# Attention and a mixture of experts on one core: 128-row operands for the first two fp32 score products, Relu on ScalarE, and a new order of steps

## The chip, the cores and the metric

The kernel runs on one core of one Trainium2 chip. The core has a matrix engine (TensorE, PE in the profile, with its weight loads shown apart as PEld), a vector engine (VectorE, DVE), an activation engine (ScalarE, ACT), a general engine (GpSimd, POOL) and an engine that issues the DMA transfers (SyncE, SP). Each works through a queue of its own in order and waits on semaphores for the others. The metric is the time of one execution in microseconds on the device; lower is better. TensorE's clock is gated: the profile gives the granted share of full speed.

## The reference

Eight batches of eight heads, 576 positions, 64 numbers per head. First an attention with a bias from running sums, then on its output a mixture of four experts, each with an attention of its own; the two best experts of a position are added up.

```python
scores = scale * np.matmul(q, k.transpose(0, 1, 3, 2))
s_pos = np.maximum(s, 0.0)
cum = np.cumsum(s_pos, axis=-1)
bias = -(cum[:, :, :, None] - cum[:, :, None, :])
scores = np.where(causal, -1000000000.0, scores + np.minimum(bias, 0.0))
attn = softmax(scores)          # with the maximum taken off first
x = attn @ v                    # heads side by side: 8 x 576 x 512
...
logits = x @ w_gate
for e in range(E):              # E = 4
    q, k, v = x @ wq[e], x @ wk[e], x @ wv[e]
    ye = causal_softmax(scale * q @ k.T) @ v @ wo[e]
    # added to out with the gate's weight where e is one of the two best
```

All numbers are fp32.

## The kernel before

**Slots.** The work is cut into pairs of heads (or of experts). A pair is a slot n; there are 48 and two empty ones, N = 50. The first four slots are the four head pairs of batch 0. From batch 1 on each batch brings four attention slots and two expert slots of the batch before.

**What a slot does.** q and k come transposed, 64 numbers on 64 partitions. Below them stand helper rows: three rows with the running sums of Relu(s) on the side of k against rows of ones on the side of q, so that the product adds the bias, and one row with minus the maximum of each query. The steps have short names, which the list ORDER uses as `slot:step`:

- `m0` to `m5` (function `maxima`, L730): bf16 products mx of 64 queries with the keys, in six PSUM banks; `M0` to `M5` (L744): VectorE reduces them to the maxima (its by-product goes to the tile sink, which nobody uses). `mt` (L764) turns the maxima with a TensorE transpose, `mA` (L768) copies them on ScalarE, `mq` (L774) sends them by DMA into the minus-maximum row of q.
- `s0` to `s5`, `s6` (function `scores`): the score products, keys as weights. From slot 2 on they are split into two rounded products (L799 on 128 rows, L804 on 97). Slots 0 and 1, the list DIRECT, take the raw fp32 q and k in one product of 68 rows (64 of q and k, 3 of sums, 1 of minus maximum) from a tile `whole` (L793, and L831 for the tails of 64 keys): this needs none of the splitting (`l0` to `l3`, `h0` to `h3`, `lq`, `lk`) with which the other slots begin.
- `E0` to `E6`: exp on ScalarE; `b`, `d`: causal masks and row sums on GpSimd; `v`, `V`: products with v (L910) and their copy.

**Before the first slot.** `c0` loads s, `c1` takes Relu and scales (L451, on VectorE), `c2` scans, `c3` and `c4` split the sums into three bf16 parts (L463, L466). `hc` sends them into the helper rows of a slot (two transfers for a slot of DIRECT, L630), `cu` to DRAM for later slots. `i0` to `i39` are spare TensorE products (L1372): they multiply the tile sink with itself and nobody reads the result. GpSimd fills constants: `k1`, `q1` the helper rows of `whole`, `f00` to `f22` those of the split tiles, `ca`, `id`, `lc` masks and the identity.

**What sets the order.** The program is written out once, with no loop at run time: `order` reads ORDER from left to right and each step issues its instructions to the engines' queues at that place. PSUM has eight banks that are taken and given back in the order of this list, and a tile's buffers are reused in the same order, so the list decides both the place in each queue and which waits there are.

The functions that the change touches, and what calls them:

Of the kernel before, what the change touches and what calls it, by code (L numbers as in the profile page):

```python
# [13 lines left out]
OP = mybir.AluOpType  # L14
# [25 lines left out]
def pieces(kt, q0, q1):  # L40
# [280 lines left out]
)  # L321

def order(pairs):
    for x in ORDER.split():
        n, step = x.split(":")
        yield int(n), step


COPY_Q, COPY_K = 3, 9
DIRECT = (0, 1)
RX = 67
SPARE = 40

FB = [0, 8, 10, 12]
NQK1 = 2
NQK2 = 3
RC = 96
RM = 96  # L340


@with_exitstack
def tile_attention_then_moe(ctx, tc, qk, vm, vt, s, wqk, wvg, wo, out):
    nc = tc.nc
# [1130 lines left out]
```

## Time and profile before

| | |
|---|---|
| median of 3 runs | 678.92 us (678.58 to 679.16) |
| profiled execution | 679.76 us, span of its instructions 677.9 us |
| busy share of the span | PE 97%, DVE 77%, ACT 69%, POOL 62% |
| mean granted TensorE clock | 0.970 |
| DMA | 81.23 MB, mean 120 GB/s |

The span runs from the first to the last instruction. A row of a timeline gives start, length, engine, line, operation, output and inputs; a group of like instructions in a row has its count behind an x. A row of windows gives the stretch, its length, for each engine the busy time in it and the count, and then the granted clock, the share of the DMA engines and GB/s. Lines are those of the kernel before.

### The profile page before, as it was taken

To read this page: it belongs to the slowest core of one execution; us is meant where nothing else is said; L and a number is where in the kernel's file an instruction comes from. 1 tells how busy PE (TensorE), PEld (TensorE's weight loads), DVE (VectorE), ACT (ScalarE), POOL (GpSimd) and SP (SyncE) were. 2 spreads that over 40 slices of the span, in tenths; PEclk is the share of its full clock that TensorE was granted. 3 is DMA by queue.
4 is the path that set the end of the run, shared out by engine and by line. 5 is a ranking of instruction groups with operands and counts; after the bars stand their busy time and mean duration, and the time that the engine had idled before them with its cause. 6 is when DMAs were issued, how large, how long until landed. Compare 5 with 4: busy or idle time off the path is not lost.

```text
span 677.9 us, 16595 instructions
## 1 busy us (share of the span) xinstructions
PE 658.2 (97%) x5906; PEld 539.1 (80%) x5906; DVE 525.1 (77%) x1449; ACT 470.8 (69%) x1090; POOL 417.9 (62%) x557
## 2 busy tenths in 40 slices
PE   6789999999999999999999989999999999999997
PEld 2456778878987888878887878888888888889885
DVE  6387787788978867986689867889677976773894
ACT  2166978787678686777677846888667876675573
POOL 7069858768766648755868537758757665808130
PEclk9559999999999999999999989999999999999999
DMA  4513544433544535555446343637363544331413
GB/s 96 164 54 108 167 134 118 109 104 96 144 109 136 146 92 144 139 172 141 120 129 160 107 124 108 175 107 157 89 193 92 137 126 111 75 84 51 121 33 124
DMA packets 48917, 81.23 MB, mean 120 GB/s; under 512 B 19246, under 2 KB 19246, under 8 KB 48836
## 3 DMA queue, kind: packets, MB, share of 16 engines
q1 hardware_dynamic: 48836, 80.18, 44.6%
q8 instruction: 47, 0.77, 0.5%
q14 instruction: 34, 0.28, 0.1%
HBM read 44.55 MB, written 10.09 MB: 81 GB/s over the span
## 4 chain that ended last, share of the span: by engine, by line
PE 85%; ACT 5%; DVE 3%; DMA 3%; issue 1%; SPq 1%; ACTq 0%; DVEq 0%
PE pvp L910 18%; PE pq L1140 13%; PE s L799 11%; PE s L804 10%; PE mx L730 8%; PE pw L1140 8%; PE po L1140 7%; PE sm L963 4%; PE s L793 2%; PE s L841 1%; ACT k L673 1%; PE po L1114 1%; ACT p L820 1%; DVE s_r L451 1%; DVE sink L744 1%
## 5 line engine op out<-in xcount | busy, mean ns | idle before, releaser
L744 DVE CUSTOM_DVE_ANT_0 sink<-mx,mask 128x64 bf16<-128x64 f32 (+7 forms) x432 | 168.9, 428 | 61.7 <-PE mx L730 50.7
L820 ACT ACTIVATE p<-s 128x512 f32<-128x512 f32 x288 | 160.1, 590 | 49.7 <-PE s L804 31.1
L853 POOL TENSOR_SCALAR_AFFINE_SELECT p<-p 128x256 f32<-128x256 f32 (+1 forms) x192 | 95.6, 507 | 157.6 <-ACT p L820 130.9
L799 PE MATMUL s<-q,k 128*128 128x320 f32 (+2 forms) x552 | 153.1, 301 | 1.2 <-DMA q<-q 0.6
L804 PE MATMUL s<-q,k 97*128 97x320 f32 (+2 forms) x552 | 141.7, 291 | 0.2 <-DMA q<-mr 0.2
L874 POOL TENSOR_TENSOR r<-r,p 128x640 f32<-128x640 f32 x92 | 129.6, 1409 | 4.5
L799 PEld LDWEIGHTS s<-q,k 128*128 128x128 f32 x552 | 105.4, 191 | 13.7 <-issue 5.0
L704 DVE TENSOR_TENSOR q<-raw,q 64x576 fp32r<-64x576 f32 x92 | 87.3, 962 | 31.4 <-ACT q L669 13.5
L1140 PE MATMUL pq<-x,wqkh 128*128 128x288 f32 x512 | 106.8, 302 | 1.8 <-ACT raw L1158 1.8
L804 PEld LDWEIGHTS s<-q,k 97*128 97x128 f32 x552 | 105.4, 191 | 1.0 <-DMA q<-mr 0.5
L910 PE MATMUL pvp<-p,v 128*64 128x320 f32 (+3 forms) x1024 | 102.9, 325 | 0.0
L730 PE MATMUL mx<-k,q 96*64 96x512 bf16 (+7 forms) x920 | 90.2, 298 | 0.4 <-ACT q L669 0.3
L710 DVE TENSOR_TENSOR k<-raw,k 64x1024 fp32r<-64x1024 f32 (+1 forms) x92 | 80.9, 890 | 12.3 <-DMA k<-k 6.7
L1140 PEld LDWEIGHTS pq<-x,wqkh 128*128 128x128 f32 x512 | 81.9, 190 | 3.9 <-ACT raw L1158 2.0
L910 PEld LDWEIGHTS pvp<-p,v 128*64 128x64 f32 x1024 | 63.1, 137 | 21.1 <-issue 2.4
L1140 PE MATMUL pq<-x,wqkl 128*128 128x288 f32 x256 | 75.9, 296 | 0.0
L871 POOL TENSOR_TENSOR r<-p 128x384 f32<-128x384 f32 x46 | 50.2, 1092 | 28.2 <-ACT p L820 28.2
L730 PEld LDWEIGHTS <-q 96*64 96x64 bf16 x920 | 47.4, 112 | 24.6 <-issue 9.2
L673 ACT ACTIVATE k<-raw 64x1024 fp32r<-64x1024 f32 (+1 forms) x92 | 61.9, 680 | 6.8 <-DMA raw<-in_qk_dram 5.1
L669 ACT ACTIVATE q<-raw 64x576 fp32r<-64x576 f32 x92 | 62.0, 679 | 0.9
L924 ACT ACTIVATE pv<-pvp 128x256 f32<-128x256 f32 (+1 forms) x92 | 36.7, 405 | 25.0 <-PE pvp L910 24.6
L1140 PE MATMUL pw<-wvgh,x 128*128 128x260 f32 x256 | 51.8, 288 | 0.0
(140 smaller groups left out, 1172.5 us busy)
## 6 DMA issues: line engine op xcount, KB each, us to landing
raw<-in_qk_dram SPq DMA_DIRECT2D x30, 576.0 KB
rb<-rr SPq DMA_DIRECT2D x92, 144.0 KB
q<-q SPq DMA_DIRECT2D x45, 288.0 KB
k<-k SPq DMA_DIRECT2D x39, 288.0 KB
v<-in_vm_dram SPq DMA_DIRECT2D x32, 256.0 KB
out_dram<-o SPq DMA_DIRECT2D x32, 256.0 KB
q<-mr SPq DMA_DIRECT2D x92, 2.2 KB
whole<-in_qk_dram SPq DMA_DIRECT2D x8, 144.0 KB
```

The costliest lines, as they stand in the source:

```text
L673: nc.scalar.activation(part(k2[0:64]), get_raw(n)[64:128, :, k], AF.Copy)
L704: nc.vector.tensor_tensor(a[64:128, j], get_raw(n)[0:64, j], q2[0:64, j].bitcast(F32), op=OP.subtract)
L710: nc.vector.tensor_tensor(part(c[0:64]), get_raw(n)[64:128, :, k], part(c[64:128]).bitcast(F32), op=OP.subtract)
L730: nc.tensor.matmul(t[64 * j : 64 * j + 64, c0 : c0 + k1 - k0], q2[0:rc, 64 * qt : 64 * qt + 64], keys(n, rc, j, k0, k1).bitcast(BF16)[:, 1 ...
L744: nc.vector.tensor_tensor_reduce(sink[:, c0 : c0 + w], t[:, c0 : c0 + w], mask[:, m0 : m0 + w], scale=1.0, scalar=mcol[n][:, 9:10] if bi = ...
L799: nc.tensor.matmul(t[0:nk, c0 : c0 + q1 - q0], K1[r1(n)][:, span(j, k0, k0 + nk)], Q1[r1(n)][:, j, q0:q1], start=True, stop=False,)
L804: nc.tensor.matmul(t[0:nk, c0 : c0 + q1 - q0], keys(n, RM + 1, j, k0, k0 + nk), Q2[r2(n)][0 : RM + 1, j, q0:q1], start=False, stop=True,)
L820: nc.scalar.activation(ptile[n][:, x % 2, 512 * ci : 512 * ci + 512], tl[x], AF.Exp, scale=0.125)
L853: nc.gpsimd.affine_select(out=a if kt else running()[:, :, 0:128], in_=a, pattern=[[64 if kt == 4 else 0, 2], [1, nk]], compare_op=OP.is_g ...
L874: add(r[:, :, q0:S], r[:, :, q0:S], p[:, :, 1024 + c : 1024 + c + S - q0], op=OP.add)
L910: nc.tensor.matmul(cur[h][64 * j : 64 * j + 64, q0 - PVC[h] : q1 - PVC[h]], vsl(j, kt), rtile[n][:, j, 0:128] if own else ptile[n][:, j, c ...
L1140: nc.tensor.matmul(t[0:nk, 0:w], l, r, start=(x == 0), stop=(x == len(terms) - 1))
```

## The change

Slots 0 and 1 get a tile `plain` in place of `whole`, in the layout of the split tiles, with all 128 partitions filled: q has ones in rows 64 to 95 and zeros in 96 to 127, k has zeros and ones there; the three rows of sums stand in k's rows 64 to 66 and minus the maximum in q's row 96. The score products take all 128 rows (68 before), mx takes 96 (67 before), and the tails of both heads are one product of 128 by 128 instead of two of 64 by 64. The constants are set by `z0`, `z1` on VectorE and `z2`, `z3` on GpSimd, in place of `q1`, `k1`. Because k's tails lie apart in the new layout, the sums go in with four transfers for a slot instead of two; q and k take three in place of four. Relu goes to ScalarE. The spare products are 60 instead of 40. ORDER is new from end to end; two of its lines, and the rest of the difference:

```diff
 ORDER = (
-    "-2:i12 -2:i17 -2:k1 -2:id -2:i9 -2:i19 -2:i8 -2:i24 -2:c0 -2:i38 -2:i32 -1:ld 0:h3 -2:c1 "
+    "-2:i37 -2:i18 -2:i23 -2:i7 -2:i21 -2:i39 -2:i12 -2:i31 -2:f12 -2:i9 -2:i30 -2:i22 -2:f20 "
...
-RX = 67
-SPARE = 40
+SPARE = 60
...
         def positive():
             t["r"] = sb.tile([P, S], F32, tag="pv", name="s_r", bufs=5)
-            nc.vector.tensor_scalar(t["r"][:n], t["s"][:n], 0.0, 8.0, op0=OP.max, op1=OP.mult)
+            nc.scalar.activation(t["r"][:n], t["s"][:n], AF.Relu, scale=8.0)
...
-    whole = {}
+    plain = {}
+
+    def whole(n):
+        if n not in plain and n < 2:
+            w = sb.tile([P, 2, 2, 2, S], F32, tag="x", name="plain", bufs=1)
+            for m in range(2):
+                plain[m] = w[:, m, 0], w[:, m, 1].rearrange("p j s -> p (j s)")
...
+        return plain[n]
...
-        def rows(x):
-            nc.gpsimd.memset(both()[64:96, 2 * x : 2 * x + 2], 1.0)
-
         def sums_in():
             for j in range(2):
                 hd = 2 * i + j
-                nc.sync.dma_start(both()[64:67, 2 + j], early[0][hd : hd + 1])
-
-        def fetch(x, j):
-            nc.sync.dma_start(both()[0:64, 2 * x + j], qk[b, 2 * i + j, 64 * x : 64 * x + 64])
...
+                for k in (slice(0, 512), slice(512, S)):
+                    nc.sync.dma_start(
+                        keys(n)[64:67, span(j, k.start, k.stop)], early[0][hd : hd + 1, :, k]
+                    )
+
+        def fetch(x):
+            part, k = PARTS[x]
+            nc.sync.dma_start(part(keys(n)[0:64]), heads[64:128, :, k])
...
+        items["h0"] = lambda: nc.sync.dma_start(queries(n)[0:64], heads[0:64])
+        items["h1"], items["h3"] = lambda: fetch(0), lambda: fetch(1)
+        items["z0"] = lambda: nc.vector.memset(queries(n)[64:96], 1.0)
+        items["z1"] = lambda: nc.vector.memset(queries(n)[96:128], 0.0)
+        items["z2"] = lambda: nc.gpsimd.memset(keys(n)[64:96], 0.0)
+        items["z3"] = lambda: nc.gpsimd.memset(keys(n)[96:128], 1.0)
...
-                    rc = RX if n in DIRECT else RC
                     nc.tensor.matmul(
                         t[64 * j : 64 * j + 64, c0 : c0 + k1 - k0],
-                        q2[0:rc, 64 * qt : 64 * qt + 64],
-                        keys(n, rc, j, k0, k1).bitcast(BF16)[:, 1::2],
+                        q2[0:RC, 64 * qt : 64 * qt + 64],
+                        keys(n)[0:RC, span(j, k0, k1)].bitcast(BF16)[:, 1::2],
...
-                    keys(n, RX + 1, j, k0, k0 + nk), queries(n)[0 : RX + 1, j, q0:q1],
+                    keys(n)[:, span(j, k0, k0 + nk)], queries(n)[:, j, q0:q1],
...
             if n in DIRECT:
-                for j in range(2):
-                    h = slice(64 * j, 64 * j + 64)
-                    nc.tensor.matmul(
-                        t[h, h], keys(n, RX + 1, j, 512, S), queries(n)[0 : RX + 1, j, q],
-                        start=True, stop=True,
-                    )
+                nc.tensor.matmul(
+                    t[:, 0:P], keys(n)[:, 0:P], queries(n)[:, :, q], start=True, stop=True
+                )
                 return
```

How the new list moves instructions is seen at three places. The first is the head of VectorE's queue, from its memset of sink to the split running sums (s_t is s, s_r its Relu, s_c the scan, p1 the tile that holds the three parts). Before:

```order
L374 MEMSET sink_80 128x256
L451 TENSOR_SCALAR s_r_134<-s_t_125 64x576
L456 SCALAR_TENSOR_TENSOR s_c_162<-s_r_134 64x576
L463 TENSOR_SCALAR p1_94<-s_c_162 64x576
L466 TENSOR_TENSOR s_c_162<-s_c_162,p1_94 64x576
```

and now, the same stretch:

```order
L375 MEMSET sink_80 128x256
L645 MEMSET plain_131 32x1152
L646 MEMSET plain_131 32x1152 x2
L457 SCALAR_TENSOR_TENSOR s_c_214<-s_r_153 64x576
L464 TENSOR_SCALAR p1_94<-s_c_214 64x576
L467 TENSOR_TENSOR s_c_214<-s_c_214,p1_94 64x576
```

The Relu is gone from VectorE (it is ScalarE's first instruction now), and three memsets of 32x1152 stand ahead of the scan.

The second place is TensorE behind the first transpose of maxima, mt of slot 0 (mx1 are maxima products of slot 1, s0 score products of slot 0). Before:

```order
L764 MATMUL mt0_280<-ident_74,mcol0_252 9x128
L730 LDWEIGHTS whole_111
L730 MATMUL mx1_5_282<-whole_111 64x256
L730 LDWEIGHTS whole_111
L730 MATMUL mx1_5_282<-whole_111 64x256
L730 LDWEIGHTS whole_111
L730 MATMUL mx1_5_282<-whole_111 64x64
L730 LDWEIGHTS whole_111
L730 MATMUL mx1_5_282<-whole_111 64x64
L793 MATMUL s0_2_291<-whole_111 128x320
```

and now, from the same transpose on:

```order
L772 MATMUL mt0_289<-ident_74,mcol0_251 9x128
L738 LDWEIGHTS plain_131
L738 MATMUL mx1_3_301<-plain_131 64x512
L738 LDWEIGHTS plain_131
L738 MATMUL mx1_3_301<-plain_131 64x512
L1376 LDWEIGHTS sink_80
L1376 MATMUL i46_306<-sink_80 128x512
```

Before, a bank of maxima products stood between mt and the first score product; now there are 13 spare products among the maxima products there, and 7 more follow inside slot 0's scores, as here:

```order
L1376 MATMUL i44_387<-sink_80 128x512
L800 MATMUL s0_4_389<-plain_131 128x320
L800 MATMUL s0_4_389<-plain_131 128x192
L1376 LDWEIGHTS sink_80
L1376 MATMUL i54_392<-sink_80 128x512
L1376 LDWEIGHTS sink_80
L1376 MATMUL i58_396<-sink_80 128x512
L800 MATMUL s0_5_404<-plain_131 128x320
```

In this stretch of TensorE's queue no spare product stood before; all 40 came ahead of the first mx.

The third place is VectorE from the last reduction of slot 0 to the first of slot 1 in the new kernel (mcol are the maxima, q1 and k1 the remainders of the split q and k of slots 2 and 3):

```order
L752 ISA sink_80,mcol0_251<-mx0_4_275,mask_79,mcol0_251 128x512
L752 ISA mcol0_251 128x1
L713 TENSOR_TENSOR q1_0_64<-raw2_155,q2_2_70 64x576
L645 MEMSET plain_131 32x1152
L719 TENSOR_TENSOR k1_1_67<-raw3_314,k1_1_67 64x128
L719 TENSOR_TENSOR k1_1_67<-raw3_314,k1_1_67 64x1024
L713 TENSOR_TENSOR q1_1_65<-raw3_314,q2_0_68 64x576
L719 TENSOR_TENSOR k1_0_66<-raw2_155,k1_0_66 64x1024
L752 ISA sink_80,mcol1_413<-mx1_0_362,mask_79 128x448
```

Before, the reductions of slot 1 followed those of slot 0 directly; now a memset of the ones of slot 1 (`z0`) and five subtractions stand between them. On GpSimd the order is now: fills of two split tiles, the mask, `z2` and `z3` of slot 0, the small memsets of `lc`, the identity, three fills of 32x1152 (`f21`, `f11`, `f01`) and `z2` of slot 1.

More of the change, by code (lines that the diff above doesn't have):

```diff
@@ L600, in tile_attention_then_moe, with keys @@
     PARTS = (main, slice(0, 512)), (tails, slice(512, S))
-    whole = {}
-    def queries(n):
-        return whole[n][:, 0:2] if n in DIRECT else Q2[r2(n)]
-    def keys(n, rows, j, k0, k1):
-        if n in DIRECT:
-            return whole[n][0:rows, 2 + j, k0:k1]
-        return K2[r2(n)][0:rows, span(j, k0, k1)]
+    plain = {}
[4 more added lines that the diff above has]
+                plain[m] = w[:, m, 0], w[:, m, 1].rearrange("p j s -> p (j s)")
+        elif n not in plain:
+            q, k = (sb.tile([P, 2, S], F32, tag="raw", name=f"plain{n}{x}", bufs=3) for x in "qk")
+            plain[n] = q, k.rearrange("p j s -> p (j s)")
+        return plain[n]
+    def queries(n):
+        return whole(n)[0] if n in DIRECT else Q2[r2(n)]
+    def keys(n):
+        return whole(n)[1] if n in DIRECT else K2[r2(n)]
     def direct(n):
         _, b, i = pairs[n]
+        heads = qk[b, 2 * i : 2 * i + 2].rearrange("h p s -> p h s")
         items = {}
-        def both():
-            if n not in whole:
-                w = sb.tile([P, 8, S], F32, tag="x", name="whole", bufs=1)
-                for y, m in enumerate(DIRECT):
-                    whole[m] = w[:, 4 * y : 4 * y + 4]
-            return whole[n]
-        def rows(x):
-            nc.gpsimd.memset(both()[64:96, 2 * x : 2 * x + 2], 1.0)
         def sums_in():
@@ L629, in sums_in, with sums_later @@
                 hd = 2 * i + j
-                nc.sync.dma_start(both()[64:67, 2 + j], early[0][hd : hd + 1])
-        def fetch(x, j):
-            nc.sync.dma_start(both()[0:64, 2 * x + j], qk[b, 2 * i + j, 64 * x : 64 * x + 64])
-        items["hc"] = sums_in
-        for x in range(2):
-            items["qk"[x] + "1"] = lambda x=x: rows(x)
-            for j in range(2):
-                items[f"h{2 * j + x}"] = lambda x=x, j=j: fetch(x, j)
+                for k in (slice(0, 512), slice(512, S)):
[5 more added lines that the diff above has]
+            nc.sync.dma_start(part(keys(n)[0:64]), heads[64:128, :, k])
+        def sums_later():
+            nc.sync.dma_start(keys(n)[64:67], cum[b * NP1 + i])
+        items["hc"] = sums_in if n < 2 else sums_later
+        items["h0"] = lambda: nc.sync.dma_start(queries(n)[0:64], heads[0:64])
[4 more added lines that the diff above has]
+        items["z3"] = lambda: nc.gpsimd.memset(keys(n)[96:128], 1.0)
         return items
@@ L771, in rows @@
         def rows():
-            at = RX if n in DIRECT else RM
             for j in range(2):
                 nc.sync.dma_start(
-                    queries(n)[at : at + 1, j].bitcast(F32),
+                    queries(n)[RM : RM + 1, j].bitcast(F32),
                     t[1][:, 64 * j : 64 * j + 64].bitcast(F32),
@@ L805, in seg @@
                 t[0:nk, c0 : c0 + q1 - q0],
-                keys(n, RM + 1, j, k0, k0 + nk), Q2[r2(n)][0 : RM + 1, j, q0:q1],
+                K2[r2(n)][0 : RM + 1, span(j, k0, k0 + nk)], Q2[r2(n)][0 : RM + 1, j, q0:q1],
                 start=False, stop=True,
@@ L828, in tail @@
             if n in DIRECT:
-                for j in range(2):
-                    h = slice(64 * j, 64 * j + 64)
-                    nc.tensor.matmul(
-                        t[h, h], keys(n, RX + 1, j, 512, S), queries(n)[0 : RX + 1, j, q],
-                        start=True, stop=True,
-                    )
+                nc.tensor.matmul(
+                    t[:, 0:P], keys(n)[:, 0:P], queries(n)[:, :, q], start=True, stop=True
+                )
                 return
```

512 rows, old and new, of the table ORDER are left out of this document.

## The prediction

> **What bounds the kernel now.** I read the page first (busy time, the clock row, the chain), then a table of windows over the whole span, then TensorE's own timeline of the first 60 us, and last the engines that TensorE waits for there.
>
> ```profile
> span 677.9 us, 16595 instructions
> PE 658.2 (97%) x5906; PEld 539.1 (80%) x5906; DVE 525.1 (77%) x1449; ACT 470.8 (69%) x1090; POOL 417.9 (62%) x557
> PEclk9559999999999999999999989999999999999999
> PE 85%; ACT 5%; DVE 3%; DMA 3%; issue 1%; SPq 1%; ACTq 0%; DVEq 0%
> ```
>
> TensorE is the bound nearly everywhere. But the clock row has a dent in its second and third digit: half speed, at the start alone. The windows (columns: span, busy time of PE, PEld, DVE, ACT, POOL, granted clock, DMA share, GB/s) say how much there is to win and where:
>
> ```profile
> 0.00:60.00 60.00, 48.31 (x228) 28.70 (x229) 38.84 (x100) 21.54 (x41) 32.00 (x55) 0.69 0.38 104
> 360.00:420.00 60.00, 58.18 (x516) 48.89 (x516) 46.12 (x130) 40.77 (x97) 35.89 (x47) 0.97 0.48 127
> 600.00:660.00 60.00, 59.72 (x501) 51.60 (x501) 42.50 (x109) 39.91 (x103) 23.66 (x37) 1.00 0.25 68
> 660.00:678.00 18.00, 13.97 (x82) 10.26 (x78) 9.10 (x20) 6.71 (x15) 0.00 (x0) 1.00 0.34 117
> ```
>
> Of 19.7 us of TensorE idle time (677.9 - 658.2), 11.7 lie in the first 60 us and 4.0 in the last 18; the 600 us between hold 4.0. So what the change does to the first 60 us is what counts. TensorE there (start, length, instruction; in brackets the idle time before it):
>
> ```profile
> 1.34 11.13 PE L1372 MATMUL i<-sink 128*128 128x512 bf16 x40 [1.34 <-DVE sink L374]
> 16.93 3.94 PE L730 MATMUL mx<-whole 67*64 67x448 bf16 x22 [4.45 <-DMA whole<-p]
> 22.76 0.37 PE L764 MATMUL mt<-ident,mcol 128*9 128x128 f32 x1 [1.89 <-DVE mcol L744]
> 25.48 5.46 PE L793 MATMUL s<-whole 68*128 68x320 f32 x12 [1.94 <-DMA whole<-mr]
> 30.87 1.92 PE L730 MATMUL mx<-whole 67*64 67x448 bf16 x14
> 32.93 5.49 PE L793 MATMUL s<-whole 68*128 68x256 f32 x12
> 39.62 0.37 PE L764 MATMUL mt<-ident,mcol 128*9 128x128 f32 x1 [1.20 <-DVE mcol L744]
> 43.40 7.16 PE L793 MATMUL s<-whole 68*128 68x256 f32 x16 [0.86 <-DMA whole<-mr]
> 50.99 2.38 PE L910 MATMUL pvp<-p,v 128*64 128x320 f32 x12
> 54.98 1.99 PE L793 MATMUL s<-whole 68*128 68x320 f32 x8
> 57.18 1.08 PE L730 MATMUL mx<-k,q 96*64 96x384 bf16 x12
> 59.05 0.42 PE L799 MATMUL s<-q,k 128*128 128x320 f32 x1
> ```
>
> The last row, the first split score product of slot 2, is my marker: from there on TensorE runs without gaps, so what the marker moves, the end moves. When is the clock half? Two rows of weight loads, then three windows:
>
> ```profile
> 5.59 0.15 PEld L1372 LDWEIGHTS <-sink 128*128 128x128 bf16 x1 [0.28 <-issue]
> 6.01 5.97 PEld L1372 LDWEIGHTS <-sink 128*128 128x128 bf16 x28 [0.28 <-issue]
> 16.00:16.50 0.50, 0.00 (x0) 0.00 (x0) 0.00 (x0) 0.00 (x0) 0.00 (x0) 0.82 0.05 14
> 26.00:38.00 12.00, 12.00 (x42) 8.42 (x40) 5.51 (x20) 6.10 (x11) 0.00 (x0) 0.50 0.34 87
> 53.50:54.00 0.50, 0.50 (x10) 0.29 (x8) 0.00 (x0) 0.00 (x0) 0.42 (x2) 0.63 0.00 0
> ```
>
> The spare products come every 0.42 us up to 6.01 us and every 0.213 us (5.97 / 28) after: 128-row work has lifted the clock within 4.7 us. It falls at 16.32 us (a mean of 0.82 over half a us is 0.32 at full and 0.18 at half clock), 3.8 us after the last spare product. Then TensorE is busy for all of 26 to 38 us, with products on 67 and 68 rows, and the clock stays at 0.50; it rises at 53.87 (the 0.63), 2.9 us after the first products on 128 rows (L910, at 50.99).
>
> **The change part by part.** (a) *128 rows for the score products of slots 0 and 1* (L793, L831). The column counts stay, so the cost of one product at a given clock I take as equal. Nearest rows: at half clock 5.46 us for 12, at full clock 1.99 us for 8 (0.455 and 0.249 us each), all on 68 rows; the ends are 0 and, if 128 rows cost a tenth more, +1.2 us on 48 records. What it buys is the clock. Busy time from the last spare product to the marker, mx (L730) and s (L793):
>
> ```profile
> 12.48:59.05 46.57, 11.84 (x90) 5.95 (x90) 0.60 0.32 94
> 12.48:59.05 46.57, 20.11 (x48) 14.21 (x48) 0.60 0.32 94
> ```
>
> s: 40 records run at half clock (5.46 + 5.49 + 7.16 = 18.11 us); at 0.249 they need 10.0: -8.1 us. mx: 11.84 less the 1.08 that is already fast is 10.8; 137 ns each at half clock (1.92 / 14) against 90 (1.08 / 12) saves a third: -3.7. The 2.38 us of L910, a third: -0.8. Together **-12.6 us** if the clock is full for all of it.
>
> In sentences that the sum does without: the Trainium skill, "TensorE: Matmul & The Clock Gate" (Part 1), states that the gate opens after one window of about 3.4 us in which TensorE was busy, and counts time, not work. Its window agrees (16.32 to 53.87 us is 11 times 3.41), its busyness does not: 12 us without a gap on 68 rows left the clock at 0.50. By that page rows are no matter, whatever kept the clock low would stay, and (a) would give nothing; this is the third rival.
>
> (b) *20 more spare products*, 13 between the first mt and the first s, 7 between the s products of slot 0: 20 x 0.213 = **+4.3 us** of TensorE work; double at half clock.
>
> (c) *Relu to ScalarE, constants to VectorE, the chain to the first mx.*
>
> ```profile
> 1.01 0.27 DVE L374 MEMSET sink<- 128x256 uint32 x1
> 3.64 6.36 DVE L451 TENSOR_SCALAR s_r<-s_t 64x576 f32<-64x576 f32 x1 [2.35 <-DMA s_t<-in_s_dram]
> 10.04 1.35 DVE L456 TENSOR_TENSOR_SCAN s_c<-s_r 64x576 f32<-64x576 f32 x1
> 13.29 0.49 DVE L463 TENSOR_SCALAR p<-s_c 64x576 int32<-64x576 int32 x1
> 13.82 0.75 DVE L466 TENSOR_TENSOR p<-s_c,p 64x576 f32<-64x576 f32 x1
> 7.47 0.68 ACT L669 ACTIVATE q<-raw 64x576 fp32r<-64x576 f32 x1
> 3.55 2.05 POOL L625 MEMSET whole<- 32x1152 f32 x2
> 9.54 0.93 POOL L426 MEMSET p<- 64x64 f32 x4
> 14.65 1.60 SPq L630 DMA_DIRECT2D whole<-p x2
> ```
>
> The Relu took 6.36 us on VectorE for a shape that costs ScalarE 0.68: it stood until GpSimd's memsets of 32x1152 ended (3.55 to 9.54). ScalarE has nothing before its first raw tile, so it ends at 3.64 + 0.68 = 4.3. VectorE now has three memsets of 32x1152 ahead of the scan, 1.05 us each by GpSimd's row (1.15 scaled up from the 0.27 of 256 elements): 1.28 + 3.15 = 4.4. Scan 1.35, two splits of 0.49 + 0.75: 8.3 us, against 14.57 before. The sums then go to each slot in four transfers instead of two; SP issues one in 0.80 us, the first mx product pair needs the third, and landing took 0.68 beyond the issue (16.93 - 16.25): 8.3 + 2.4 + 0.7 = 11.4. The 40 early spares end at 12.48, so mx starts at **12.5 instead of 16.93**, without a gap. Behind the four transfers wait slot 1's q and k, which have until 19 us. The unknown is the splits: a TENSOR_SCALAR like the Relu, and GpSimd now runs four 32x1152 memsets from 8 to 12 us by its new order. No wait is one end; the other is 8 to 12 us spent waiting, as the Relu did: sums at 13.3, mx at 16.4. I take no wait, since the second split comes at about 7.1 among GpSimd's short memsets (like the 9.54 row, where the Relu got through).
>
> A page in passing: the Trainium skill, "SBUF — State Buffer" (Who interferes with whom), gives the shared ports to whichever starts first for one whole instruction, which would hold a split 1.05 us at most, and mx at 13.1. The 6.36 us, six memsets long, does not fit that.
>
> (d) *Idle time.* The brackets above sum to 10.3 us before the marker; all go. New ones: mx of slot 0, 20 products, now lasts 20 x 0.09 = 1.8 us, to 14.3, while the first reduction
>
> ```profile
> 18.22 0.62 DVE L744 CUSTOM_DVE_ANT_0 sink<-mx,mask 128x448 bf16<-128x448 f32 x1 [3.65 <-PE mx L730]
> 37.19 0.75 DVE L704 TENSOR_TENSOR q<-raw,q 64x576 fp32r<-64x576 f32 x1
> 47.73 2.52 DVE L704 TENSOR_TENSOR q<-raw,q 64x576 fp32r<-64x576 f32 x2
> ```
>
> started 1.29 us after the first mx and mt 5.83 after it; VectorE's time stays, so mt comes at 12.5 + 5.83 less 0.6 of clock = 17.7: 3.4 idle. Behind mt, slot 1's first mx waits for a memset of its ones (z0), queued on VectorE after a subtraction: 0.75 + 1.05, so 1.6 idle, to 19.5. Only then come the spares, so the minus-max transfer (2.7 us from mt to s before) is hidden under them. Last, the spares read sink, which the reductions write: slot 1's first reduction now waits for the last spare, four score banks (4.0 us) before the end of s, and takes about 4.4: 0.7 idle. Sum 5.7 new, 10.3 gone: **-4.6**.
>
> (e) *The clock between 12.5 and 19.5.* Sparse mx and 4.6 us of gap are what dropped it before. I expect it at half when the spares start and full again some 3.5 to 4.5 us later: about 9 spares cost 0.21 more each: **+2.0**. Ends: 0, and (third rival) all of it.
>
> (f) *VectorE behind.* Its work until the marker stays and grows by four memsets, in a shorter time; subtractions beside GpSimd work took 1.26 instead of 0.75. Ends 0 and 8 x 0.51 = 4.1; I take **+1.0**, as the reductions of slot 2 have about 1 us of slack in the new order.
>
> (g) *The other 600 us.* Every engine's order is new, but 4.0 us of idle time is all it can win (with the half-clock stretch that the 0.97 shows, 2 more). It can lose as much by one or two more such stalls. I take 0, ends -5 and +4. The two tail products of slot 0 and 1 becoming one: nothing, 4 short records each.
>
> Sum: -12.6 + 4.3 - 4.6 + 2.0 + 1.0 = -9.9 us. The profiled execution took 679.76 us (span 677.9 and 1.9 around it), 0.8 over the median of 678.92; that offset cancels: 678.9 - 9.9 = **669.0 us**.
>
> **The rivals.** *1, the clock never drops.* For it: only 7 us pass between spares and spares. Against: the fall at 16.3 needed 3.8 us. Without (e) and (f): 666.0. *2, the sums are late* behind GpSimd's memsets, as the Relu was: mx at 16.4, 3.9 us more idle: 672.9. *3, the clock stays at half* until the pv products, because it is not the rows that hold it down. For it: nothing on this chip's trace shows an s product on 128 rows in fp32. Against: L910 is fp32 too and the clock rose under it. Then the -12.6 is lost, the spares cost 20 x 0.428 = 8.6, and mx of slot 0 at half clock fills about 1.9 of the new idle time: 8.6 - 4.6 - 1.9 = +2.1, 681.0, slower. It decides if the clock is still 0.50 at 30 us. *4, the new order of the rest stalls* once or twice more (1.8 us of idle plus a stretch at half clock each): 672 to 676.
>
> **How the numbers follow.** Forecast 0.52 (666 to 671), rival 1 0.15, rival 2 0.13, rival 3 0.06, rival 4 0.10, and 0.04 for a rest so much worse that nothing is left. Low end: rival 1 with part of (g)'s gain, 662; high end: rival 2 with 2.5 of (g)'s loss, 675. Less than 0.2% (1.4 us) can't be told from no change here. Slower: rival 3 and part of the last, 0.07; same 0.03; faster 0.90.
>
> **What would show it.** Relu on ACT near 3.7 us and 0.7 long; mx from about 12.5; clock 0.50 for no more than about two slices and full by 25 us; s records on 128 rows at about 0.25 us; marker near 48 to 49 us instead of 59; idle after the marker as before. Wrong if the splits on VectorE last several us, if the clock is half under 128-row s products, or if TensorE's idle time between 60 and 660 us grows past 8 us.

## The result, and the profile after

The changed kernel takes 661.79 us (median of 4 runs, 660.42 to 662.79) against 678.75 us (677.98 to 679.16) for the kernel before: a ratio of 0.975, 95% interval 0.9728 to 0.9772. It is faster, as forecast, but by 17.0 us where 9.9 were forecast, and it lies just under the low end of the range (662). The execution in the trace took 661.08 us, 18.7 less than the one traced before: that one lies 1.0 above its median, this one 0.7 below.

The same rows of the page as those shown of before, now of after (span, busy times, TensorE's clock in 40 slices, the chain by engine):

```profile
span 659.4 us, 16622 instructions
PE 645.2 (98%) x5921; PEld 531.6 (81%) x5922; DVE 508.8 (77%) x1452; ACT 471.6 (72%) x1091; POOL 414.9 (63%) x557
PEclk9799999999999999999999999999999999999999
PE 94%; DVE 2%; ACT 1%; DMA 1%; issue 0%; SPq 0%; DVEq 0%; ACTq 0%
```

The dent in the clock row is one shallow digit instead of two 5s. TensorE is busy 13 us less, and its idle time fell from 19.7 to 14.2 us. By windows:

```profile
0.00:60.00 60.00, 50.55 (x346) 30.53 (x347) 41.58 (x127) 32.67 (x62) 41.11 (x69) 0.94 0.46 122
360.00:420.00 60.00, 60.00 (x571) 51.55 (x571) 47.93 (x126) 45.60 (x105) 37.23 (x49) 1.00 0.49 128
600.00:642.00 42.00, 41.41 (x387) 34.46 (x389) 30.75 (x84) 25.08 (x65) 14.41 (x23) 1.00 0.28 75
642.00:660.00 18.00, 13.33 (x66) 9.33 (x62) 8.19 (x20) 6.68 (x15) 0.00 (x0) 0.98 0.31 104
```

The first row is what the change was expected to move. The second was a surprise: before, this stretch had 1.8 us of idle time and a clock of 0.97; now it has neither. A choice of rows from TensorE's timeline of the front:

```profile
11.42 0.39 PE L738 MATMUL mx<-plain 96*64 96x448 bf16 x1
12.69 1.60 PE L738 MATMUL mx<-plain 96*64 96x448 bf16 x19 [0.88 <-DMA plain<-p]
17.77 0.37 PE L772 MATMUL mt<-ident,mcol 128*9 128x128 f32 x1 [3.49 <-DVE mcol L752]
19.67 0.64 PE L738 MATMUL mx<-plain 96*64 96x512 bf16 x2 [1.52 <-DVE plain L645]
28.01 1.03 PE L800 MATMUL s<-plain 128*128 128x320 f32 x4
32.74 3.72 PE L800 MATMUL s<-plain 128*128 128x320 f32 x16 [1.67 <-ACT p L827]
39.35 3.69 PE L800 MATMUL s<-plain 128*128 128x256 f32 x16
48.74 0.38 PE L806 MATMUL s<-q,k 128*128 128x256 f32 x1
```

The last row is the marker: 48.74 us where it was 59.05, 10.3 us earlier, against 9.9 forecast. Some terms of the front, in the order of the forecast: the score products up to the marker and the late spares (two rows of windows for these products alone: TensorE, weight loads, clock, DMA), ScalarE's Relu, VectorE's two splits and the last subtraction (it ends at 9.10, when the sums are ready):

```profile
12.50:48.74 36.24, 11.73 (x48) 8.57 (x48) 0.91 0.37 106
19.00:32.00 13.00, 7.41 (x19) 2.20 (x20) 0.79 0.42 112
3.64 0.68 ACT L452 ACTIVATE s_r<-s_t 64x576 f32<-64x576 f32 x1 [1.55 <-DMA s_t<-in_s_dram]
6.54 0.47 DVE L464 TENSOR_SCALAR p<-s_c 64x576 int32<-64x576 int32 x1
7.83 0.48 DVE L464 TENSOR_SCALAR p<-s_c 64x576 int32<-64x576 int32 x1
8.35 0.75 DVE L467 TENSOR_TENSOR p<-s_c,p 64x576 f32<-64x576 f32 x1
```

The spans of the two traces differ by 18.5 us. Cut at the marker, first before, then after:

```profile
0.00:59.05 59.05, 47.36 (x221) 27.75 (x221) 37.92 (x98) 21.48 (x40) 31.05 (x54) 0.68 0.38 102
59.05:677.90 618.85, 610.82 (x5687) 511.39 (x5685) 487.18 (x1352) 449.29 (x1050) 386.86 (x504) 1.00 0.46 122
```

```profile
0.00:48.74 48.74, 39.29 (x232) 21.46 (x233) 32.13 (x95) 22.62 (x41) 30.25 (x55) 0.93 0.44 117
48.74:659.40 610.66, 605.92 (x5691) 510.16 (x5689) 476.66 (x1358) 449.01 (x1050) 384.69 (x503) 1.00 0.47 124
```

Ahead of the marker TensorE's busy time fell by 8.1 us and its idle time by 2.2. Behind it lie 8.2 us, where the forecast had put nothing: its idle time fell by 3.3 us (8.0 to 4.7), and its busy time, for the same products, by 4.9. The experiments therefore have two questions: are the front's terms what they were said to be, and where do the other us come from?

### The profile page after: what moved, and what is told of

It is laid out like the page before. It is cut to its first block, busy times and chain, and to the rows that moved or that the text cites. A ratio compares the mean times of both kernels' runs of the same rounds, so it can differ in the third digit from the quotient of the medians.

```text
span 659.4 us, 16622 instructions
## 1 busy us (share of the span) xinstructions
PE 645.2 (98%) x5921; PEld 531.6 (81%) x5922; DVE 508.8 (77%) x1452; ACT 471.6 (72%) x1091; POOL 414.9 (63%) x557
## 4 chain that ended last, share of the span: by engine, by line
PE 94%; DVE 2%; ACT 1%; DMA 1%; issue 0%; SPq 0%; DVEq 0%; ACTq 0%
PE pvp L914 20%; PE pq L1144 16%; PE s L806 11%; PE s L811 11%; PE mx L738 10%; PE pw L1144 8%; PE po L1144 7%; PE sm L967 4%; PE s L845 1%; PE s L800 1%; PE po L1118 1%; PE mt L772 1%; PE i L1376 1%; DMA q<-mr 1%; PE gt L1256 1%
## 5 line engine op out<-in xcount | busy, mean ns | idle before, releaser
L857 POOL TENSOR_SCALAR_AFFINE_SELECT p<-p 128x256 f32<-128x256 f32 (+1 forms) x192 | 90.8, 481 | 126.5 <-ACT p L827 103.7
L806 PE MATMUL s<-q,k 128*128 128x192 f32 (+2 forms) x552 | 151.9, 299 | 0.0
L811 PE MATMUL s<-q,k 97*128 97x192 f32 (+2 forms) x552 | 141.6, 291 | 0.7 <-DMA q<-mr 0.6
L878 POOL TENSOR_TENSOR r<-r,p 128x640 f32<-128x640 f32 (+1 forms) x92 | 128.6, 1398 | 4.8
L914 PE MATMUL pvp<-p,v 128*64 128x128 f32 (+3 forms) x1024 | 100.6, 322 | 0.0
L713 DVE TENSOR_TENSOR q<-raw,q 64x576 fp32r<-64x576 f32 x92 | 81.7, 905 | 20.1 <-ACT q L678 14.1
L738 PE MATMUL mx<-k,q 96*64 96x256 bf16 (+7 forms) x920 | 87.1, 293 | 0.0
L875 POOL TENSOR_TENSOR r<-p 128x384 f32<-128x384 f32 x46 | 47.8, 1038 | 38.6 <-ACT p L827 35.1
L682 ACT ACTIVATE k<-raw 64x128 fp32r<-64x128 f32 (+1 forms) x92 | 61.4, 680 | 10.1 <-DMA raw<-in_qk_dram 5.8
L857 POOL TENSOR_SCALAR_AFFINE_SELECT r<-p 128x256 f32<-128x256 f32 x48 | 31.5, 655 | 35.4 <-ACT p L827 35.4
```

What stands on the lines that cost most here:

```text
L713: nc.vector.tensor_tensor(a[64:128, j], get_raw(n)[0:64, j], q2[0:64, j].bitcast(F32), op=OP.subtract)
L738: nc.tensor.matmul(t[64 * j : 64 * j + 64, c0 : c0 + k1 - k0], q2[0:RC, 64 * qt : 64 * qt + 64], keys(n)[0:RC, span(j, k0, k1)].bitcast(BF ...
L806: nc.tensor.matmul(t[0:nk, c0 : c0 + q1 - q0], K1[r1(n)][:, span(j, k0, k0 + nk)], Q1[r1(n)][:, j, q0:q1], start=True, stop=False,)
L811: nc.tensor.matmul(t[0:nk, c0 : c0 + q1 - q0], K2[r2(n)][0 : RM + 1, span(j, k0, k0 + nk)], Q2[r2(n)][0 : RM + 1, j, q0:q1], start=False, ...
L857: nc.gpsimd.affine_select(out=a if kt else running()[:, :, 0:128], in_=a, pattern=[[64 if kt == 4 else 0, 2], [1, nk]], compare_op=OP.is_g ...
L878: add(r[:, :, q0:S], r[:, :, q0:S], p[:, :, 1024 + c : 1024 + c + S - q0], op=OP.add)
```

## Experiments

Each comparison is with the kernel before, run beside it; its median was 678.4 to 680.0 us.

### Which of the rows, the Relu and the list does it?

`before_rows`: the kernel before and its own list, with the 128-row operands and what their layout needs (four transfers of sums for a slot, four memsets more on VectorE).

```diff
- keys(n, RX + 1, ...), queries(n)[0 : RX + 1, ...]    # 68 rows
+ keys(n)[:, ...], queries(n)[:, ...]                  # 128 rows; z0..z3 fill the constants
  ...
  ORDER: the old one (z0, z2 for q1, k1; z1, z3 behind -2:c4 and -1:M4)
```

> The old kernel with the 128-row operands alone: old list of steps, Relu on VectorE, 40 spare products, the constants of rows 96 to 127 set on VectorE where it waits anyway. Theory R (a window counts as busy by the rows in use): the clock rises one or two windows of 3.4 us after the first score products, near 30 to 33 us instead of 53.9, so some 30 of their 48 records take 0.25 instead of 0.455 us: about -6 us, 672 to 673 us. Rival (the rows do not matter, something else kept the clock low): clock half until 53 us as before, 679 us.

Measured 679.48 us, ratio 0.9998 (0.9975 to 1.0021): nothing. Two windows and two rows of its trace tell why:

```profile
28.00:32.00 4.00, 4.00 (x10) 3.05 (x10) 0.00 (x0) 1.28 (x2) 0.00 (x0) 0.50 0.59 150
32.00:34.00 2.00, 1.83 (x17) 0.89 (x16) 0.81 (x5) 0.00 (x0) 0.00 (x0) 0.92 0.30 108
41.10 0.27 PE L755 MATMUL mt<-ident,mcol 128*9 128x128 f32 x1 [3.56 <-DVE mcol L735]
44.88 2.58 PE L783 MATMUL s<-plain 128*128 128x256 f32 x5 [2.01 <-DMA plain<-mr]
```

The clock does rise under the 128-row score products, 4.7 us after the first of them (27.64 us). In the front it is half for 23.9 us instead of 37.6, and TensorE's busy time falls by 7.7 us (658.2 to 650.5). But its idle time grows by 8.6 (19.7 to 28.3). The largest wait is that of slot 1's mt (41.10) for VectorE, whose old order puts subtractions of later slots between the reductions. A part is the layout's own: the first score product comes at 27.64 us where it came at 25.48, after two waits of 0.83 and 0.84 us for transfers into plain that the kernel before does not have. So the rows work; in the old list waits take their gain back.

`before_relu` (the Relu alone, old list) and `after_relu_dve` (all but the Relu).

```diff
- nc.vector.tensor_scalar(t["r"][:n], t["s"][:n], 0.0, 8.0, op0=OP.max, op1=OP.mult)
+ nc.scalar.activation(t["r"][:n], t["s"][:n], AF.Relu, scale=8.0)     # after_relu_dve: the reverse
```

> The old kernel with Relu on ScalarE and nothing else. The first maxima product comes when the 40 spare products end, at about 12.5 instead of 16.9 us: -4.4 us. Theory R: the clock still falls, since the maxima and 68-row products do not count as busy, and stays at half to about 50 us: 674 to 675 us. Rival (the 4.4 us gap alone dropped the clock): the clock stays full through the score products, 662 to 666 us.

> The new kernel with Relu back on VectorE, at the same place of the list. Theory A (the Relu stands until GpSimd's series of 32x1152 memsets ends, here at about 6.4 us): the sums are ready some 3 us later, maxima at about 15.5 us, +3 us: about 665 us. Rival (GpSimd's memsets leave gaps now, the Relu takes 0.5 us): +1 us at most, 662 to 663 us.

Measured 676.23 us (ratio 0.995, 0.9932 to 0.9968), and 662.38 us (661.66 to 665.48), that is 0.6 more than the changed kernel. The Relu in both, first `before_relu` (with what ScalarE does ahead of it), then `after_relu_dve`:

```profile
6.50 0.31 ACT L673 ACTIVATE k<-raw 64x128 fp32r<-64x128 f32 x1 [4.41 <-DMA raw<-in_qk_dram]
6.83 0.68 ACT L451 ACTIVATE s_r<-s_t 64x576 f32<-64x576 f32 x1
```

```profile
3.72 0.50 DVE L452 TENSOR_SCALAR s_r<-s_t 64x576 f32<-64x576 f32 x1 [1.12 <-DMA s_t<-in_s_dram]
```

On ScalarE in the old list the Relu queues behind a rounding that waits for its transfer until 6.50. So the first mx comes at 14.51 us and not at 12.5, a gap of 2.35 us is left ahead of it, and the clock falls and stays half as before: the rival, that without the gap it would stay full, was not put to the test. The marker moves by 1.6 us, to 57.43; the rest of the 2.9 lies behind it. On VectorE in the new list the Relu takes 0.50 us instead of 6.36, since GpSimd's long memsets start only at 4.28 there. The new list, not the engine, took the 6 us away.

### Does the row count hold the clock down?

`after_68`: the changed kernel with 68 and 67 rows read in slots 0 and 1.

```diff
+ rc = 67 if n in DIRECT else RC                       # maxima
- q2[0:RC, ...], keys(n)[0:RC, ...]
+ q2[0:rc, ...], keys(n)[0:rc, ...]
  ...
- keys(n)[:, ...], queries(n)[:, ...]                  # score products
+ keys(n)[0:68, ...], queries(n)[0:68, ...]
  ...                                                  # minus the maximum in row 67
```

> The new kernel with 68 rows (67 for the maxima) of its operands used in slots 0 and 1, minus the maximum in row 67; layout, list, spare products and Relu as in the new kernel. Theory R: the spare products lift the clock at about 24 us, but it falls again under the 68-row products after the last spare one (31 us) and stays half to the products with v of slot 1: +6 to +8 us, 668 to 670 us. Rival (once lifted, any busy TensorE holds it): 662 us.

Measured 666.74 us (665.63 to 669.54), 5.0 more, where theory R said 6 to 8; its ratio to the kernel before, 0.9818 (0.979 to 0.9845), lies clear of 0.975 (0.9728 to 0.9772). The same two windows in the changed kernel and, below, in `after_68`:

```profile
32.00:34.00 2.00, 1.26 (x6) 1.03 (x7) 1.93 (x12) 1.30 (x4) 0.00 (x0) 1.00 0.02 4
34.00:42.00 8.00, 7.90 (x61) 6.04 (x60) 7.55 (x20) 3.92 (x7) 5.83 (x8) 1.00 0.20 66
```

```profile
32.00:34.00 2.00, 0.76 (x2) 0.56 (x3) 1.93 (x13) 1.70 (x4) 0.00 (x0) 0.63 0.01 4
34.00:42.00 8.00, 8.00 (x23) 5.50 (x23) 4.07 (x11) 2.54 (x5) 2.10 (x3) 0.50 0.00 0
```

The spares had lifted the clock to 1.00 in both (26 to 32 us). Both have a pause of 1.67 us ahead of the third score group. With 68 rows the clock falls at its end (32.5 us) and stays at 0.50 while TensorE is busy in 8.00 of 8.00 us; with 128 it does neither. The fall alone could be chance (a pause of one length does not always bring one, as is seen below); that it stays is what tells. The third rival (it is not the rows) is out. How many rows are enough, no run tells. The Trainium skill's "TensorE: Matmul & The Clock Gate" (Part 1) lets busy time alone open the gate; this row disagrees with it, and the measurement decides.

### Are the spare products worth their time?

`after_nospare`: `SPARE = 60` back to 40, so that the 20 new steps fall out of the list. Timed in two comparisons.

> The changed kernel without the 20 new spare products (SPARE back to 40, list otherwise the same). In the changed kernel they keep TensorE busy from 20.24 us to the score products, at half clock to 24.3 us. Theory A, the spares are not needed: 128-row score products lift the clock by themselves. Score products then start at about 22 us instead of 25.78 but run their first one or two windows of 3.4 us at half clock: clock half to about 25-29 us, 660 to 662.5 us. Theory B, without spares the mixture of sparse maxima and score products stays under what lifts the clock: half to 35 us or more, at least 4 us lost, 665 to 670 us.

> The changed kernel without the 20 new spares once more, beside the two kernels below: 658.3, as in its first comparison.

Measured 658.29 us (0.9719, 0.9687 to 0.9752) and 659.85 us (0.9723, 0.9695 to 0.9752): by medians 2 to 3.5 us *faster* than with them, below the range of theory A. The intervals of the ratios overlap with that of the changed kernel (0.9728 to 0.9772), but seven of the eleven executions without the spares are shorter than the shortest of the four with them (660.42). Windows and products of the first comparison's trace:

```profile
24.00:26.00 2.00, 2.00 (x9) 1.19 (x6) 1.99 (x3) 1.87 (x5) 0.00 (x0) 0.50 0.59 160
26.00:32.00 6.00, 4.11 (x19) 3.21 (x18) 5.67 (x23) 5.04 (x9) 0.00 (x0) 0.94 0.01 2
22.48 0.77 PE L836 MATMUL s<-plain 128*128 128x128 f32 x2 [1.45 <-DMA plain<-mr]
45.12 0.38 PE L806 MATMUL s<-q,k 128*128 128x256 f32 x1
```

The first score product comes at 22.48 us instead of 25.78, and the 128-row products bring the clock up by themselves, some 2.1 us later than with spares (26.7 against 24.6). The marker is at 45.12 instead of 48.74. In the trace of `after_nospare_2` the clock is full only from 29.1 us, and the marker stands at 45.12 all the same: TensorE's products are slower there, and its wait for ScalarE's p ahead of 30.37 us is 0.71 us instead of 1.89. So there the clock is not what sets the marker.

The 3.6 us at the marker are not all won at the end. The traced execution of `after_nospare` took 661.58 us, the longest of its five and 0.5 more than the trace of the changed kernel: behind the marker TensorE is idle for 7.9 us instead of 4.7, with waits of 1.33 us at 216.95 (for VectorE) and 1.55 at 231.52 (for a minus-maximum transfer). `after_nospare_2` (660.77) has one of 1.71 at 229.27. Slots that start earlier meet waits that the changed kernel does not have there.

`after_mask`: the late spares read the mask instead of sink, so that slot 1's first reduction no longer waits for them. `after_plus`: besides, z0 of slot 1 earlier and 12 more spares ahead of mt.

```diff
+ w = sink if x < 40 else mask[:, 0:512]
- nc.tensor.matmul(t, sink[:, 0:P], sink, start=True, stop=True)
+ nc.tensor.matmul(t, w[:, 0:P], w, start=True, stop=True)
  # after_plus, in ORDER: "-1:z0" ahead of "-2:m0"; "-2:i60" to "-2:i71" behind "-1:m3"
```

> The changed kernel with the 20 late spare products multiplying the mask tile instead of the tile sink, so that slot 1's first reduction on VectorE (which writes sink) no longer waits for the last spare (3.79 us until 31.11). Theory A: that wait is what makes TensorE idle for 1.67 us before 32.74 us; it goes and the time falls by 1.5: 660.3. Rival: the score banks then wait for ScalarE or GpSimd just as long and nothing is won: 661.8.

> As after_mask, and further: the memset of slot 1's ones (z0) stands ahead of slot 0's reductions, in the 4.1 us in which VectorE waits for the first mx, and 12 more spare products (on the mask tile) stand ahead of mt in the 3.49 us in which TensorE waits for the reductions. Theory A: the clock no longer falls to half for 17.5 to 24.3 us (2.3 us of TensorE time), z0's 1.5 us and the spare wait's 1.67 us go: about 656. Rival: what follows mt is set by ScalarE, GpSimd and the minus-maximum transfer, not by TensorE's clock: 659 to 661.5. If the 12 spares hold up mt instead: 662 or more.

Measured 661.52 us (659.71 to 663.13) and 662.72 us (658.16 to 666.03): nothing won. `after_mask` is its rival; `after_plus` lies 1.2 above its rival's range, though the 12 spares did not hold up mt (17.79 against 17.77). `after_mask`, VectorE, TensorE, and ScalarE between two exponentials:

```profile
27.21 0.62 DVE L752 CUSTOM_DVE_ANT_0 sink<-mx,mask 128x448 bf16<-128x448 f32 x1
32.74 1.67 PE L800 MATMUL s<-plain 128*128 128x320 f32 x6 [1.67 <-ACT p L827]
29.07 0.60 ACT L827 ACTIVATE p<-s 128x512 f32<-128x512 f32 x1 [1.71 <-PE s L800]
29.57 0.67 ACT L678 ACTIVATE q<-raw 64x576 fp32r<-64x576 f32 x1
30.26 1.25 ACT L682 ACTIVATE k<-raw 64x1024 fp32r<-64x1024 f32 x2
31.53 0.68 ACT L678 ACTIVATE q<-raw 64x576 fp32r<-64x576 f32 x1
32.12 0.57 ACT L827 ACTIVATE p<-s 128x512 f32<-128x512 f32 x1
```

The reduction starts at 27.21 instead of 31.11, and TensorE waits 1.67 us just the same: it waits for a score bank, which the exponential at 32.12 gives back, and that stands behind 2.6 us of roundings in ScalarE's queue. In `after_plus` the clock is full until 25 us and half for one window instead of two, z0's wait is gone, and the marker still moves only to 47.98: the minus-maximum transfer (first score product at 22.46) and the same 1.67 us at 32.36 take it back.

`nospare_e5` and `nospare_e53` move those exponentials ahead of the roundings.

```diff
  ORDER of after_nospare:
- 0:s4 0:E4 1:h0 0:lv -1:z3 1:h1 1:h3 0:s5 1:l1 2:h2 0:E5 1:w0h -1:M0 0:s3 0:E3
+ 0:s4 0:E4 0:s5 0:E5 1:h0 0:lv -1:z3 1:h1 1:h3 1:l1 2:h2 1:w0h -1:M0 0:s3 0:E3
  # nospare_e53: 0:s3 0:E3 right behind 0:E5 as well
```

> As after_nospare, with the steps 0:s5 and 0:E5 right behind 0:E4, so that on ScalarE three roundings of q and k for a later slot (1:h0, 1:h1, 1:h3, together 2.6 us) no longer stand between two exponentials. Theory A: these roundings, not the spares, are what TensorE's wait of 1.7 to 1.9 us (before 30.38 us, put down to ScalarE's p) is for; it shrinks to what is left before the third exponential: 1 to 1.9 us faster than after_nospare, 656.4 to 657.3. Rival: the roundings, half a us to a us later, make a later maximum or score product wait instead: 658.3.

> As nospare_e5, with 0:s3 and 0:E3 moved too, ahead of the three roundings and of a weight rounding. Theory A: the wait of 1.9 us goes: 656.4. Rival: the roundings are now 1.2 us later and something waits for them: 658.3 or more.

Measured 658.19 us (657.14 to 659.35; ratio 0.9705, 0.9677 to 0.9733) and 660.50 us (657.22 to 666.89), beside `after_nospare_2` at 659.85. The rivals, both times. In `nospare_e5` the wait is still there, one group of products later, and the marker moves from 45.12 to 45.02:

```profile
31.74 1.13 PE L785 MATMUL s<-plain 128*128 128x256 f32 x4 [1.54 <-ACT p L812]
45.02 0.38 PE L791 MATMUL s<-q,k 128*128 128x256 f32 x1
```

In `nospare_e53` no wait is left among slot 0's score products, but the products with v then wait 1.43 us for p (at 33.60), and the marker comes at 45.77. That speaks for the amount of ScalarE's work there, and not its order, as what sets the pace; no run takes work away from ScalarE. `nospare_e5` has the lowest median of all, 20 us under the kernel before; from `after_nospare` it can't be told.

### Where do the us behind the marker come from?

`before_td` moves one step in the old list: the gate columns of slot 27, for whose transfer a copy out of PSUM on ScalarE waited 4.41 us.

```diff
- ... 27:T1 ...            29:E5 27:td 31:ld ...
+ ... 27:T1 27:td ...      29:E5 31:ld ...
```

> The old kernel with one step moved: the transfer of the gate columns of slot 27 (td) is issued right after the copy that it reads (T1), and no longer behind the transfer of slot 29's sums. Theory A: TensorE's stall of 1.82 us near 401 us and the 3.4 us at half clock after it go, -1.8 - 1.7 = -3.5 us: about 675.3 us, and the clock row has no dent there. Rival: something else is late next at the same place and the time stays at 678.8 us.

Measured 676.08 us (ratio 0.997, 0.9942 to 0.9998): -2.7 us by medians, with an interval that just leaves out zero. TensorE and ScalarE in the kernel before, and one window of before and of `before_td`:

```profile
401.59 0.54 PE L1140 MATMUL pq<-x,wqkh 128*128 128x288 f32 x2 [1.82 <-ACT raw L1158]
401.12 0.71 ACT L1158 ACTIVATE raw<-pq 128x288 f32<-128x288 f32 x2 [4.41 <-DMA gcol<-g]
399.00:407.00 8.00, 6.18 (x39) 6.01 (x35) 3.44 (x8) 2.66 (x5) 0.00 (x0) 0.79 0.32 87
```

```profile
399.00:407.00 8.00, 8.00 (x66) 7.56 (x65) 6.44 (x19) 4.86 (x11) 1.16 (x4) 1.00 0.52 126
```

A pause of 1.82 us and a stretch of 3.4 us at half clock behind it: both are gone with the one step. That the pause brings the half-clock stretch with it is not sure, though. `before_relu` has the same pause, and its clock stays full:

```profile
399.47 0.54 PE L1140 MATMUL pq<-x,wqkh 128*128 128x288 f32 x2 [1.94 <-ACT raw L1158]
397.00:405.00 8.00, 6.06 (x47) 5.89 (x47) 4.70 (x14) 4.25 (x9) 0.43 (x2) 1.00 0.30 82
```

So the step may be worth 1.8 us in some executions and 3.5 in others; the 2.7 of the medians lies between.

Hybrid lists: `h1_s3`, `h1_s8`, `h1_s30` have the new list up to slot 3's, 8's or 30's first score step and the old order of the remaining steps; `h1_s8_td` moves 27:td in it besides; `h2_s3` is the kernel before with the old list up to slot 3's score products and the new order from there.

```diff
+ ORDER = new[:new.index("8:s0")] + [x for x in old if x not in the first part]     # h1_s8
```

> The new kernel, but its list of steps is followed only up to the first score step of slot 3; all steps not done by then follow in the order of the old list. The marker (first split score product of slot 2) was reached 10.3 us earlier by the change, the end 18.5 us earlier, so 8.2 us came after it. Theory A, those 8.2 us belong to the new list of the later slots: 661.8 + 8 = about 670 us, with the old stall of 1.8 us and its stretch at half clock back. Theory B, the later slots are faster only because the engines enter them further ahead: 662 to 664 us, no stall.

> The mirror image: the old kernel (68 rows, Relu on VectorE, 40 spare products) with the old list up to a score step of slot 3, and from there the order of the new list. Theory A: 678.8 - 8 = about 671 us, marker still at 59 us. Theory B: 677 to 679 us.

> The changed kernel with the new list up to slot 30's first score step and the old list's order of steps from there (about 405 us on; the old list's stall at 400 us lies in the part that is new). With the cut at slot 3 the old rest cost 6.8 us. Theory A, the gain of the rest lies where the old list stalls, in the first slots after the marker and around 400 us: no more than 1.2 us lost here, 661.8 to 663. Rival, it is spread evenly over the 600 us (fewer small waits at each change of kind): 255/600 of 8.2 us lost, 665.3.

> The changed kernel with the new list up to slot 8's first score step and the old list's order of steps from there (the old list's stall at 400 us is in). With the cut at slot 3 the old rest cost 6.8 us, with the cut at slot 30 it cost 1.6. Theory A, the gain after the marker is made of the slots right behind it (3 to 8) and of the stall at 400 us: 1.1 to 3.5 us lost here, 663 to 665. Rival, it is spread over the whole rest: 668.

> As h1_s8, with the step 27:td of the old part right behind 27:T1, as in before_td, where it took the stall at 400 us away and 2.7 us with it. Theory A: nothing of the gain is left to lose but the 1.6 us of the cut at slot 30: 662 to 663.5. Rival, spread evenly: 665.5 to 666.

| kernel | median, us | ratio (95%) | against after |
|---|---|---|---|
| h1_s3 | 668.60 | 0.986 (0.9807 to 0.9912) | +6.8 |
| h1_s8 | 664.11 | 0.9777 (0.9748 to 0.9807) | +2.3 |
| h1_s8_td | 663.29 | 0.976 (0.9735 to 0.9785) | +1.5 |
| h1_s30 | 663.38 | 0.9782 (0.9749 to 0.9814) | +1.6 |
| h2_s3 | 673.84 | 0.9939 (0.9907 to 0.9972) | -4.9 to before |

The old order of the rest costs 6.8 us on top of the new front. 4.5 of them lie in slots 3 to 7 (`h1_s3` less `h1_s8`), and 2.3 in the 550 us after that, where an even spread would have left 6. The old pause at the gate columns is shorter in these lists (1.08 us in `h1_s3`, 1.15 in `h1_s8`) and lowers no clock. Of the 4.5, one wait is made by the splice itself (`h1_s3`):

```profile
59.80 0.42 PE L723 MATMUL mx<-k,q 96*64 96x448 bf16 x3 [1.66 <-ACT q L663]
```

and of the rest the 36 us from the marker on show a part (sums of six windows, first before, then after):

```profile
sum 36.00, PE 35.14 PEld 25.65 DVE 29.75 ACT 32.05 POOL 27.48; mean PE 5.86 PEld 4.28 DVE 4.96 ACT 5.34 POOL 4.58
```

```profile
sum 36.30, PE 36.30 PEld 26.71 DVE 30.50 ACT 32.92 POOL 29.18; mean PE 6.05 PEld 4.45 DVE 5.08 ACT 5.49 POOL 4.86
```

TensorE does not run without gaps from the marker on in the kernel before: 0.9 us of 36 are idle, against none. Idle time is not all of it. From the marker to the end TensorE is busy for 609.5, 608.3 and 609.1 us in `before_td`, `before_relu` and `h1_s3`, which have the old order there, and for 605.7 to 605.9 in the changed kernel, `after_mask` and `after_relu_dve`, which have the new one, with as many products (4 records apart at most) and no half-clock stretch in any of the six (606.4 to 606.9 in four more kernels of the new order). So some 3 us are gaps between products that are too short to be counted as idle, or products that run longer; no run tells which. `h2_s3` has a wait of its own (1.77 us at 243.93, for a minus-maximum transfer, and a half-clock stretch after it), so its -4.9 is likely less than the new order of the rest is worth.

`after_switch`: in the new list 27 steps of pv products stand behind the next maxima, so that TensorE changes its kind of product 54 times more.

```diff
- ... 7:v4 7:lq 8:m4 8:m3 ...      (27 places of this kind)
+ ... 7:lq 8:m4 7:v4 8:m3 ...
```

> The new kernel with 27 products-with-v steps from slot 4 on moved behind the next maxima step, so that TensorE changes its kind of product 54 times more often (693 times in the list in place of 639), with the same work. Theory A: a change between mx and pv costs TensorE about 0.1 us that is not hidden (its trace: start to start 0.10 to 0.12 us over the pace), so +5.4 us, about 667 us, busy all the same. Rival: the change is free and the time stays at 661.8 us.

Measured 662.88 us (662.12 to 664.07), +1.1, hardly clear of the changed kernel's runs (660.42 to 662.79): about 0.02 us a change, if anything. Grouping by kind is not where the gain is.

## Why the prediction was right and wrong

- **What bounds it:** right. The front could be moved by its own waits and its clock.
- **(a) 128 rows: right, as one half of it.** The 48 score products take 11.73 us up to the marker where they took 20.11: 8.4 less, forecast 8.1. `after_68` and `before_rows` show the cause, and also that the sum was wrong to price it alone: without the list it is worth nothing.
- **(b) spares +4.3 and (e) clock +2.0: the sum a little small, the sign of the step not asked.** In the trace the late spares take 7.41 us of TensorE time (19 records) against 6.3, since about half of them run at half clock. The prediction let them stand as the price of the clock; the runs without them are 2 to 3.5 us faster by medians, because 128-row products lift the clock anyway.
- **(c) the chain: right in its times** (first mx 11.42, the rest 12.69, forecast 12.5; sums at 9.1, forecast 8.3; splits 0.47 and 0.48 us, so rival 2 did not come), wrong in its cause: the new list's later memsets would have let the Relu through on VectorE as well. (The 13.1 of the aside on the ports does not follow from its rows: 11.4 + 1.05 gives 12.5.)
- **(d) idle time, -4.6: too large.** The first two new waits, 3.49 and 1.52, were forecast as 3.4 and 1.6. The third, 0.7 for the last spare, is 1.67 and is ScalarE's; 0.88 for the sums' transfer ahead of 12.69 was not forecast. Up to the marker TensorE's idle time fell from 11.69 to 9.45 us, by 2.2.
- **(f) VectorE behind, +1.0:** not seen by itself. With (d) it makes -3.6, against 2.2 measured; TensorE's busy time makes -8.1 where (a), (b) and (e) make -6.3. So the front's -9.9 against -10.3 is two misses that cancel, and its closeness is in part luck.
- **(g) the other 600 us: the step that failed.** It was put at 0, between -5 and +4, with 4.0 us of idle time and 2 of half clock as all that could be won. The runs showed 6.7 by medians (17.0 - 10.3; `h1_s3` gives 6.8) and 8.2 between the traces. Of the 8.2, 3.3 are idle time, 1.7 the half-clock stretch, and about 3 are busy time at full clock, for which the prediction had no term. By place: the pause at 400 us, with the stretch that can follow it, 2.7 by `before_td`; 2.8 in slots 3 to 7 (4.5 by `h1_s3` against `h1_s8`, 1.7 of it the splice's own wait); 1.5 beyond (`h1_s8_td`), not told from the scatter of runs (660.4 to 662.8). The error was to take the rows' idle time as all there was to win and then to forecast its middle at 0: the stall's row, with its cause (a transfer queued too late), was in the trace and could be priced at 1.8 to 3.5, and the marker was read as the place from which TensorE has no gaps, which it was not.
- **The range:** its low end, 662, was added up from rival 1, which did not come, and 4 us of (g). That the time lies only 0.2 us below it is chance.
- **Rivals:** 1 (the clock never drops) and 3 (stays half) did not come; 4 (the new rest stalls) is the opposite of what happened. The ground given for 3, that no score product on 128 rows in fp32 stands in the trace, overlooks the last row of the timeline shown there (59.05, 128*128, f32), though at a clock that was up already.
- **Open:** what makes up the 2.8 us in slots 3 to 7. The waits there are short (the longest 0.6 us), a part is busy time, and a splice adds a wait of its own. Open too is why the same products keep TensorE busy for some 3 us less in the new order.

## What to carry to other kernels

A whole new list of steps is priced at its places, not at zero: go through the old list's stalls one by one, see whether the new order keeps what causes each, and count the half-clock stretch that a pause can bring with it. Idle time is no upper bound of what a new order can win: here busy time fell as well. A cheaper product pays only if the list lets the other engines keep up; test each part of a change in the old order before crediting it. And filler that keeps the clock up has a price too: see whether the real work does it alone. An earlier front is not yet an earlier end: look for the waits that the rest meets then.

## What the runs showed of the hardware

- Gap-free products on 67 and 68 rows did not lift the clock off 0.50 (`after_68`, 34 to 42 us, TensorE busy in 8.00 of 8.00 us). On 128 rows the same products raise it (`before_rows`, 4.7 us after the first).
- A pause of 1.82 us on TensorE was followed by 3.4 us at half clock (before, ahead of 401.59); the same pause, 1.94 us long, left the clock at 1.00 in `before_relu` (ahead of 399.47). Pauses of 1.67 us (after, ahead of 32.74) and of 1.15 us (`h1_s8`, ahead of 387.86) left it at 1.00 too. So length alone does not decide; what does, these runs do not vary.
- The same Relu on VectorE took 6.36 us beside six GpSimd memsets in a row, and 0.50 us just ahead of two of them.
